# A gated-state attention chained to a cosine MoE on one core: w_in's tiles loaded with 32 or 64 rows outermost, heads p and p+4 paired, early k and r in two loads each

## The chip, the cores and the metric

The kernel runs on one core of one Trainium2 chip. The metric is device microseconds (us) of one execution, as the median of several. A profile is one execution recorded by the hardware profiler; its span, from the first instruction to the last, is a little shorter than that execution's time.

The engines have their own instruction streams and run them in order: PE (TensorE, matmuls; PEld is its weight load), DVE (VectorE), ACT (ScalarE), POOL (GpSimd) and SP (SyncE, which here only issues DMA transfers; SPq in the profile). They wait for each other through semaphores. The 16 DMA engines of the core move what the queues issue.

## The reference

r, k and v are (4 batches, 8 heads, 768 steps, 48), in float32. w_in (384 x 2048) and w_out (2048 x 384) are float64: the kernel sees every weight as two 32-bit words, so one row's piece of 128 columns is 1 KB.

```python
for t in range(S):                                   # attention, state (B, H, D, D)
    cur = np.einsum('bhd,bhe->bhde', u[None] * k[:, :, t], v[:, :, t])
    y[:, :, t] = np.einsum('bhd,bhde->bhe', r[:, :, t], state + cur)
    state = w[None, :, :, None] * state + np.einsum('bhd,bhe->bhde', k[:, :, t], v[:, :, t])
x = y.transpose(0, 2, 1, 3).reshape(B * S, H * D)    # 3072 tokens x 384
h = x @ w_in
out = (h * np.cos(h)) @ w_out
```

## The kernel before

**Attention.** Tokens come in 24 chunks of 128 (`chunk(i, ...)`). A chunk loads k, r and v, multiplies them by decays, forms an A matrix per head pair (`mm_a`, L818), and from A, v and the carried state the 384 columns of x, transposed (`mm_x`, L839 with the state and L850 with A). `mm_z` (L863) makes what the state gains: one matmul a head, 48 x 48, and the two heads of a pair go to the two halves of the output partitions. The first 12 chunks (`EARLY`) come before the MoE begins; the others are spread through it and are loaded in another way (`late`).

Heads are handled in pairs (p, j): p of 0 to 3, and j = 0 or 1 says which half of the 128 partitions a head takes. Before the change, head h = 2p + j, so heads 0 and 1 are a pair. The early chunks keep k and r in tiles of eight slots of 64 (`k`, `r_all`), pair by pair.

**Order of x's rows.** `mm_x` can write 32 rows of the output at a time, so the 384 columns of x stand in three tiles (kk) of four groups (g) of 32 rows, and a group holds pieces of heads as `x_columns(kk, g)` lists them. w_in's rows must stand in the same order on the partitions.

**MoE.** 3072 tokens go in eight blocks of 384 and w_in's 2048 columns in 16 tiles f of 128. One step is one block with one f: nine matmuls for h (L230), then the cosine gate on ACT and DVE (L241, L244, L247, L1017, L1020, L1023), then nine matmuls for the output (L236). The first four blocks take f in groups (0 to 1, 2 to 4, 5 to 9, 10 to 15), the last four take all 16 in a row.

**Weights.** `conv(i, ...)` brings tile f of w_in (even i) or w_out (odd i) into one of three raw buffers (`raw`, twice, and a part of `r_all`), and turns float64 into two float32r parts: ACT L552 and DVE L560 and L572 read the raw words, POOL L583 adds and sets the buffer free, ACT L588 writes the high part (`w_in_hi`, `w_out_hi`), DVE L593 the low part. The load is `load_raw`: w_out's tile in one DMA (L461), w_in's in eight (L446), since its rows are permuted. Near the end the weights are loaded once more for a check of their range, w_in in natural order in one DMA (L456).

**What sets the order.** `Plan` fixes one order for all engines when the kernel is built, from costs and due times written in the code. At run time every engine goes through its list in order. The framework gives SP's DMAs eight completion semaphores in turn, so that a DMA also waits for the one eight places ahead of it to land.

Of the kernel before, what the change touches and what calls it, by code (L numbers as in the profile page):

```python
# [15 lines left out]
ALU = mybir.AluOpType  # L16
# [55 lines left out]
class Plan:  # L72
# [91 lines left out]
def kernel(  # L164
# [49 lines left out]
    w_in_w = moe_w_in.bitcast(I32)  # L214
# [35 lines left out]
    with ExitStack() as actx:  # L250
# [37 lines left out]
        wr = att.tile([NP, 2, DP], F32, name="wr")  # L288
# [8 lines left out]
        dec_k = att.tile([P, H, D], F32, name="dec_k")  # L297
# [11 lines left out]
        op = plan.op  # L309
        PE, DVE, ACT, POOL, SP, ACTQ = "PE", "DVE", "ACT", "POOL", "SP", "ACTQ"  # L310
# [22 lines left out]
        def start_dve():  # L333
# [9 lines left out]
            SP,  # L343
            -200,
            0.1,
            lambda: nc.sync.dma_start(wr[:, :, 0:D], w.rearrange("(p j) d -> p j d", j=2)),
            [],
            lat=2.2,
        )
# [48 lines left out]
        b_tab = Buf(B_EARLY)  # L398
# [4 lines left out]
                nc.tensor.transpose(pt[:, p, :], decT_k[:, p, :], ident)  # L403

        def tab_copy():
            pt = b_tab().rearrange("q (p j d) -> q (p j) d", p=NP, j=2)
            nc.scalar.copy(dec_k, pt[:, :, 0:D])

        o_tt = op(PE, -6, 0.5, tab_t, [o_dtk, o_pool], [b_tab], lat=0.3)
        o_dk = op(ACT, -6, 0.45, tab_copy, [o_tt], [b_tab])  # L410
# [6 lines left out]
            lat=3.0,  # L417
# [16 lines left out]
        def load_raw(i, raw, by_x=False):  # L434
            f, part = divmod(i, 2)
            if part == 0 and by_x:
                rl = 2 * DFF
                for kk in range(NK):
                    g = 0
                    while g < 4:  # L440

                        first = x_columns(kk, g)
                        n = 2 - len(first) + 1
                        (h0, skip0), (h1, skip1) = (x for i in range(n) for _, x in x_columns(kk, g + i))
                        c0, c1 = h0 * D + max(skip0, 0), h1 * D + max(skip1, 0)
                        nc.sync.dma_start(  # L446
                            raw()[32 * g : 32 * (g + n)].rearrange("p (kk f) w -> p kk (f w)", kk=NK)[:, kk],
                            bass.AP(
                                tensor=w_in_w.tensor,
                                offset=w_in_w.offset + c0 * rl + f * P * 2,  # L450
                                ap=[[(c1 - c0) * rl, 2], [rl, 16 * n], [1, 2 * P]],
                            ),
                        )
                        g += n
            elif part == 0:
                nc.sync.dma_start(  # L456
                    raw().rearrange("p (kk f) w -> p kk (f w)", kk=NK),
                    w_in_w[:, f * P * 2 : (f + 1) * P * 2].rearrange("(kk p) f -> p kk f", p=P),
                )
            else:  # L460
                nc.sync.dma_start(raw().rearrange("p f w -> p (f w)"), w_out_w[f * P : (f + 1) * P, :])  # L461
# [48 lines left out]

        def x_columns(kk, g):

            j, m, which = (
# [3 lines left out]
            )[kk][g]  # L519
            one, two = 4 * m + j, 4 * m + j + 2  # L520
            return (((0, (one, 0)),), ((0, (two, 16)),), ((0, (one, 32)), (16, (two, -16))))[which]

# [85 lines left out]
        for t in range(2):  # L608
            for j in range(2):
                for g in range(4):  # L610
                    some = [(*x, j, kk - j, g) for kk in range(NK) for _, x in x_columns(kk, g) if x[0] % 2 == j]
                    PARTS.append(some[t])

        last_A = [None]
# [7 lines left out]
        def heads(buf):  # L622
            return buf().rearrange("q (h d) -> q h d", h=H)
# [7 lines left out]
        def chunk(i, due, xbuf):  # L631
# [14 lines left out]
            def load(buf, src):  # L646
                return lambda: nc.sync.dma_start(
                    buf()[:, :, 0:D], src[b, :, c * C : (c + 1) * C, :].rearrange("h t d -> t h d")
                )

            late = i >= EARLY
# [3 lines left out]

            rbs = [rb] if late else [rb, r_first]

            def rn():
                return heads(rb) if late else rb()[:, :, 0:D]

            def load_r():
                nc.sync.dma_start(rn(), r[b, :, c * C : (c + 1) * C, :].rearrange("h t d -> t h d"))

            def load_s(buf, src):
                def part(m, q, n_q, p, n_p, n):
                    j, d0 = m // 2, 32 * (m % 2)
                    nc.sync.dma_start(  # L670
                        staged(buf)[32 * m + q : 32 * m + q + n_q, p : p + n_p, 0:n],
                        bass.AP(
                            tensor=src.tensor,
                            offset=src.offset + ((b * H + 2 * p + j) * S + c * C + 4 * q) * D + d0,
                            ap=[[4 * D, n_q], [2 * S * D, n_p], [1, n]],
                        ),
                    )
# [12 lines left out]

                return go
# [29 lines left out]
            if late:  # L721
# [17 lines left out]
                e0,  # L739
                due - 2.8,  # L740
                c0,
                lambda: n0.tensor_tensor(heads(mb), rn(), kb()[:, :, 0:D], op=ALU.mult),
                [l_r, l_k],
                [*rbs, kb, mb],
                port=True,
# [1 line left out]
            e2, c2, n2 = on(2)  # L747

            def decay_k():
                n2.tensor_tensor(kb()[:, :, 0:D], kb()[:, :, 0:D], dec_k, op=ALU.mult)  # L750

            if not first:
                o_kd = op(e2, due - 2.7, c2, decay_k, [o_m, o_dk], [kb], port=True)
# [50 lines left out]
            def diagonal(j):  # L804
                def go():
                    for p in range(NP):
                        h = 2 * p + j
# [25 lines left out]
            def mm_x():  # L833
                if c:
                    for n, (h, skip, i, at, g) in enumerate(PARTS):
                        p, j = divmod(h, 2)
                        ps = slice(j * DP, j * DP + D)
                        e0 = p * DP + skip
                        nc.tensor.matmul(  # L839
                            xv(i)[G * g : G * g + G, at, :],  # L840
                            zc[b].rearrange("q p e -> q (p e)")[ps, e0 : e0 + G],
                            rT()[ps, p, :],
                            start=(n < 8),
                            stop=False,
                            skip_group_check=True,
                        )
                for n, (h, skip, i, at, g) in enumerate(PARTS):
                    p, j = divmod(h, 2)
                    e0 = h * DP + skip
                    nc.tensor.matmul(  # L850
                        xv(i)[G * g : G * g + G, at, :],
                        vb().rearrange("q h d -> q (h d)")[:, e0 : e0 + G],
                        A[j]()[:, p, :],
                        start=(not c and n < 8),
                        stop=True,
                        skip_group_check=True,
                    )

            def mm_z():
                z = zp()[:, 0 : NP * D].rearrange("q (p e) -> q p e", p=NP)  # L860
                for h in range(H):
                    p, j = divmod(h, 2)
                    nc.tensor.matmul(z[j * DP : j * DP + D, p, :], kb()[:, h, 0:D], vb()[:, h, 0:D], start=True, stop=True)  # L863

            more = c < CPB - 1

# [366 lines left out]
```

## Time and profile before

| | |
|---|---|
| median of 3 runs | 589.65 us (589.63 to 592.54) |
| the profiled execution | 589.45 us |
| its span | 587.7 us |
| PE busy | 527.6 us, 90% of the span |
| DVE, ACT, POOL busy | 395.6, 328.4, 178.2 us |
| loads of w_in's tiles for `conv` | 128 DMAs on SP: 64 of 64 KB, 64 of 32 KB |

The span has four stretches: to about 58 us mostly the early chunks; to 75 us their end and the first steps; from 75 to 232 us the steps of the grouped blocks while the remaining weights are loaded and converted; after that the other steps with the late chunks. Queries by windows give busy time in a stretch, the granted PE clock, and the DMA engines' mean busy share.

### The profile page before, as it was taken

How to read it: one execution, taken by the hardware profiler on the slowest of the kernel's cores; microseconds unless marked ns; L12 is line 12 of the kernel's file. 1: busy time of each engine (PE TensorE's matmuls, PEld its weight loads, DVE VectorE, ACT ScalarE, POOL GpSimd, SP SyncE). 2: the span in 40 equal slices, each digit the busy share in tenths (PEclk: the TensorE clock that was granted, in tenths of full speed). 3: DMA queues.
4: the chain of work that ended last, by engine and by line, in shares of the span. 5: the costliest groups of instructions: out<-in, count | busy, mean ns of one | idle time of the engine just before them, and what ended most of it. 6: DMA issues, size and time to landing. Idle time of an engine off the chain costs nothing.

```text
span 587.7 us, 12700 instructions
## 1 busy us (share of the span) xinstructions
PE 527.6 (90%) x4721; PEld 490.9 (84%) x4721; DVE 395.6 (67%) x820; ACT 328.4 (56%) x841; POOL 178.2 (30%) x186
## 2 busy tenths in 40 slices
PE   8979857778668796999999999999999999999994
PEld 5757647667667696999999999999999999999994
DVE  5759865664666485745677688768777877776552
ACT  3768744653545364555456657655755676565442
POOL 6566322123333133411150445043043313300000
PEclk9989959979788987999999999999999999999998
DMA  9687324345344445632536678345726662501001
GB/s 143 113 143 131 72 81 128 107 142 127 87 102 106 105 102 124 124 45 38 95 70 118 124 166 198 83 121 122 190 81 163 163 155 86 150 3 40 2 1 45
DMA packets 114984, 61.66 MB, mean 105 GB/s; under 512 B 78433, under 2 KB 110818, under 8 KB 114914
## 3 DMA queue, kind: packets, MB, share of 16 engines
q1 hardware_dynamic: 109586, 53.50, 37.4%
q0 software_dynamic: 5184, 7.08, 8.6%
q8 instruction: 38, 0.62, 0.5%
q14 instruction: 32, 0.26, 0.1%
q10 hardware_dynamic: 144, 0.20, 0.1%
HBM read 48.96 MB, written 11.80 MB: 103 GB/s over the span
## 4 chain that ended last, share of the span: by engine, by line
PE 63%; DMA 17%; SPq 7%; DVE 5%; POOL 3%; issue 2%; ACT 1%; DVEq 0%; POOLq 0%; ACTq 0%
PE bank L230 26%; PE both L236 18%; PE bank L236 9%; DMA raw<-in_moe_w_in_dram 8%; SPq L446 7%; DMA r_all<-in_moe_w_in_dram 4%; PE bank L818 3%; PE bank L850 3%; DMA r_all<-in_r_dram 2%; DMA raw<-in_moe_w_out_dram 2%; PE bank L839 1%; POOL f L583 1%; DMA r_all<-in_moe_w_out_dram 1%; DMA k<-in_k_dram 1%; PE bank L863 1%
## 5 line engine op out<-in xcount | busy, mean ns | idle before, releaser
L230 PE MATMUL bank<-xh,w_in_hi 128*128 128x384 f32 x384 | 132.5, 345 | 6.8 <-ACT w_in_hi L588 4.1
L230 PE MATMUL bank<-xh,w_in_lo 128*128 128x384 f32 x384 | 131.3, 342 | 1.6 <-DVE w_in_lo L593 1.6
L230 PE MATMUL bank<-xl,w_in_hi 128*128 128x384 f32 x384 | 131.2, 342 | 0.0
L1023 DVE TENSOR_TENSOR gl<-f,gh 128x384 fp32r<-128x384 f32 (+1 forms) x132 | 78.6, 599 | 30.2 <-ACT gh L1020 29.9
L241 ACT ACTIVATE qi<-bank 128x384 int32<-128x384 f32 (+1 forms) x132 | 62.8, 479 | 60.1 <-PE bank L230 59.6
L247 ACT ACTIVATE f<-f 128x384 f32<-128x384 f32 (+1 forms) x132 | 67.3, 513 | 44.6 <-DVE f L244 43.0
L244 DVE SCALAR_TENSOR_TENSOR f<-bank,qi 128x384 f32<-128x384 f32 (+1 forms) x132 | 70.9, 540 | 29.5 <-ACT qi L241 29.1
L236 PE MATMUL both<-w_out_hi,gh 128*128 128x384 f32 x256 | 89.1, 348 | 1.4 <-DVE f L1052 1.1
L1017 DVE TENSOR_TENSOR f<-bank,f 128x384 f32<-128x384 f32 (+1 forms) x132 | 70.9, 540 | 27.3 <-ACT f L247 25.6
L1020 ACT CAST gh<-f 128x384 fp32r<-128x384 f32 (+1 forms) x132 | 65.8, 501 | 42.0 <-DVE f L1017 35.8
L236 PE MATMUL both<-w_out_hi,gl 128*128 128x384 f32 x256 | 88.7, 346 | 0.0
L236 PE MATMUL both<-w_out_lo,gh 128*128 128x384 f32 x256 | 88.3, 345 | 0.0
L230 PEld LDWEIGHTS bank<-xh,w_in_hi 128*128 128x128 f32 x384 | 74.2, 193 | 8.8 <-ACT w_in_hi L588 4.5
L230 PEld LDWEIGHTS bank<-xh,w_in_lo 128*128 128x128 f32 x384 | 73.9, 193 | 2.2 <-DVE w_in_lo L593 2.2
L230 PEld LDWEIGHTS bank<-xl,w_in_hi 128*128 128x128 f32 x384 | 74.1, 193 | 0.0
L236 PE MATMUL bank<-w_out_hi,gl 128*128 128x384 f32 x128 | 45.5, 356 | 20.1 <-DVE gl L1023 20.1
L808 ACT ACTIVATE A<-ident,a 128x128 f32<-128x128 f32 x192 | 59.5, 390 | 4.4 <-DVE a L799 4.2
L236 PE MATMUL bank<-w_out_hi,gh 128*128 128x384 f32 x128 | 45.8, 358 | 11.9 <-ACT f L1050 6.8
L730 POOL TENSOR_TENSOR kT<-kT,decT_k 112x512 f32<-112x512 f32 x12 | 15.7, 1311 | 128.5 <-DVE kT L725 78.4
L236 PEld LDWEIGHTS both<-w_out_hi,gh 128*128 128x128 f32 x256 | 49.5, 193 | 3.1 <-DVE f L1052 1.9
L236 PEld LDWEIGHTS both<-w_out_hi,gl 128*128 128x128 f32 x256 | 49.7, 194 | 0.0
L236 PEld LDWEIGHTS both<-w_out_lo,gh 128*128 128x128 f32 x256 | 49.7, 194 | 0.0
(104 smaller groups left out, 802.6 us busy)
## 6 DMA issues: line engine op xcount, KB each, us to landing
raw<-in_moe_w_out_dram SPq DMA_DIRECT2D x22, 384.0 KB
out_dram<-f POOLq DMA_DIRECT2D x36, 192.0 KB, 5.5
raw<-in_moe_w_in_dram SPq DMA_DIRECT2D x13, 384.0 KB
k<-in_k_dram SPq DMA_DIRECT2D x24, 192.0 KB
v<-in_v_dram SPq DMA_DIRECT2D x24, 192.0 KB
out_dram<-f SPq DMA_DIRECT2D x23, 192.0 KB
r_all<-in_moe_w_out_dram SPq DMA_DIRECT2D x10, 384.0 KB
raw<-in_k_dram SPq DMA_DIRECT2D x31, 96.0 KB
```

Source lines behind the costliest of these rows:

```text
L230: nc.tensor.matmul(ph, a, b_, start=(i == 0), stop=(i == len(mm) - 1))
L236: nc.tensor.matmul(acc, a[:, ts], b_[:, f, :], start=(first and i == 0), stop=(last and i == 2))
L241: nc.scalar.activation(qi, ph, AF.Copy, scale=INV_2PI, bias=0.25)
L244: nc.vector.scalar_tensor_tensor(q, ph, INV_2PI, qi, op0=ALU.mult, op1=ALU.subtract)
L247: nc.scalar.activation(q, q, AF.Sin, scale=TWO_PI, bias=0.5 * math.pi)
L446: nc.sync.dma_start(raw()[32 * g : 32 * (g + n)].rearrange("p (kk f) w -> p kk (f w)", kk=NK)[:, kk], bass.AP(tensor=w_in_w.tensor, offset ...
L808: nc.scalar.activation(A[j]()[:, p, :], ident, AF.Copy, scale=ab()[:, h : h + 1])
L818: nc.tensor.matmul(cube(Ap[j])[:, p, :], kT()[ps, p, :], rT()[ps, p, :], start=True, stop=True)
L850: nc.tensor.matmul(xv(i)[G * g : G * g + G, at, :], vb().rearrange("q h d -> q (h d)")[:, e0 : e0 + G], A[j]()[:, p, :], start=(not c and ...
L1017: nc.vector.tensor_tensor(g()[:, cs], ph()[:, cs], q()[:, cs], op=ALU.mult)
L1020: nc.scalar.copy(gh()[:, cs], g()[:, cs])
L1023: nc.vector.tensor_tensor(gl()[:, cs], g()[:, cs], f32(gh())[:, cs], op=ALU.subtract)
```

## The change

w_in's tile comes in five DMAs in place of eight. In each, the outermost dimension of both sides is 32 or 64 rows; before, the DRAM side had two runs of 16 or 32 rows (outermost 2). For that, `x_columns` gets another order of x's columns, and that order needs heads p and p + 4 as a pair (head h = p + 4j). The tables of decays (`wr`, `dec_k`) and the late chunks' staged loads are renumbered to match. In the early chunks k and r are loaded in two DMAs each (heads 0 to 3 to the even slots, 4 to 7 to the odd ones), so that a pair stands side by side; products with v-ordered tiles read those tiles through a permuted view. `mm_z` goes through heads in their order: the four of one half of the partitions first, then the four of the other.

```diff
         def load_raw(i, raw, by_x=False):
             f, part = divmod(i, 2)
             if part == 0 and by_x:
-                rl = 2 * DFF
-                for kk in range(NK):
-                    g = 0
-                    while g < 4:
...
-                        nc.sync.dma_start(
-                            raw()[32 * g : 32 * (g + n)].rearrange("p (kk f) w -> p kk (f w)", kk=NK)[:, kk],
-                            bass.AP(
...
-                                ap=[[(c1 - c0) * rl, 2], [rl, 16 * n], [1, 2 * P]],
+                def rows(p0, n, kk, n_kk, c0, dc):
+                    rl = 2 * DFF
+                    dims = [[rl, n], [dc * rl, n_kk], [1, 2 * P]]
+                    nc.sync.dma_start(
+                        raw()[p0 : p0 + n].rearrange("p (kk f) w -> p kk (f w)", kk=NK)[:, kk : kk + 2 * n_kk - 1 : 2],
...
+                rows(32, 64, 0, 2, 0, 320)
+                rows(0, 32, 0, 2, 160, 64)
+                rows(96, 32, 0, 2, 128, 64)
+                rows(0, 64, 1, 1, 64, 0)
+                rows(64, 64, 1, 1, 256, 0)
...
+            def load_p(buf, src):
+                def go():
+                    for j in range(2):
+                        nc.sync.dma_start(
+                            buf()[:, j::2, 0:D],
+                            src[b, j * NP : (j + 1) * NP, c * C : (c + 1) * C, :].rearrange("h t d -> t h d"),
+                        )
...
-            l_k = op(SP, due - 5.2, 1.35, load(kb, k), ahead, [kb], lat=2.6, line=ln)
-            l_r = op(SP, due - 5.1, 1.35, load_r, ahead, rbs, lat=2.6, line=ln)
+            l_k = op(SP, due - 5.2, 1.35, (load if late else load_p)(kb, k), ahead, [kb], lat=2.6, line=ln)
+            l_r = op(SP, due - 5.1, 1.35, load_r if late else load_p(rb, r), ahead, rbs, lat=2.6, line=ln)
...
             def decay_k():
-                n2.tensor_tensor(kb()[:, :, 0:D], kb()[:, :, 0:D], dec_k, op=ALU.mult)
+                n2.tensor_tensor(in_turn(kb), in_turn(kb), split(dec_k), op=ALU.mult)
...
                 for h in range(H):
-                    p, j = divmod(h, 2)
-                    nc.tensor.matmul(z[j * DP : j * DP + D, p, :], kb()[:, h, 0:D], vb()[:, h, 0:D], start=True, stop=True)
+                    j, p = divmod(h, NP)
+                    at = h if late else 2 * p + j
+                    nc.tensor.matmul(z[j * DP : j * DP + D, p, :], kb()[:, at, 0:D], vb()[:, h, 0:D], start=True, stop=True)
```

PE, DVE, ACT and POOL keep their lists, instruction for instruction; only operands differ. SP's list changes in two kinds of place. The first is a weight tile in the grouped stage. Before, on SP (L446 is w_in, L461 w_out, L1063 a store of a finished block; `DMAHW` are the eight completion semaphores, `Pool` means that POOL has set the raw buffer free):

```order
L446 DMA raw_118<-in_moe_w_in_dram 64x1x256 [waits DMAHW6_49,Pool_49]
L446 DMA raw_118<-in_moe_w_in_dram 32x1x256 [waits DMAHW7_49]
L446 DMA raw_118<-in_moe_w_in_dram 32x1x256 [waits DMAHW0_49]
L446 DMA raw_118<-in_moe_w_in_dram 64x1x256 [waits DMAHW1_49]
L446 DMA raw_118<-in_moe_w_in_dram 64x1x256 [waits DMAHW2_49]
L446 DMA raw_118<-in_moe_w_in_dram 32x1x256 [waits DMAHW3_49]
L446 DMA raw_118<-in_moe_w_in_dram 32x1x256 [waits DMAHW4_49]
L446 DMA raw_118<-in_moe_w_in_dram 64x1x256 [waits DMAHW5_49]
L461 DMA raw_117<-in_moe_w_out_dram 128x768 [waits DMAHW6_49,Pool_49]
```

After, the same place on SP (L442 is w_in, L462 w_out, L1081 a store):

```order
L442 DMA raw_118<-in_moe_w_in_dram 64x2x256 [waits DMAHW7_49,Pool_49]
L442 DMA raw_118<-in_moe_w_in_dram 32x2x256 [waits DMAHW0_49]
L442 DMA raw_118<-in_moe_w_in_dram 32x2x256 [waits DMAHW1_49]
L442 DMA raw_118<-in_moe_w_in_dram 64x256 [waits DMAHW2_49]
L442 DMA raw_118<-in_moe_w_in_dram 64x256 [waits DMAHW3_49]
L462 DMA raw_117<-in_moe_w_out_dram 128x768 [waits DMAHW4_49,Pool_49]
```

Three issues are gone, and w_out's load, which stood behind a wait for the first of the eight w_in pieces, now waits for a DMA ahead of the tile.

The second place is an early chunk. Before, SP has three loads for each chunk (L647 for k and v, L665 for r; here two chunks):

```order
L647 DMA k_84<-in_k_dram 128x8x48 [waits DMAHW4_49,PE_49,Pool_49]
L665 DMA r_all<-in_r_dram 128x8x48 [waits DMAHW5_49,Pool_49]
L647 DMA v_87<-in_v_dram 128x8x48 [waits DMAHW6_49,PE_49]
L647 DMA k_85<-in_k_dram 128x8x48 [waits DMAHW7_49,PE_49,Pool_49]
L665 DMA r_all<-in_r_dram 128x8x48 [waits DMAHW0_49,DMAHW2_49,PE_49,Pool_49]
L647 DMA v_88<-in_v_dram 128x8x48 [waits DMAHW1_49,PE_49]
```

After, it has five (L655 for the halves of k and r; the same two chunks):

```order
L655 DMA k_84<-in_k_dram 128x4x48 [waits DMAHW5_49,PE_49,Pool_49]
L655 DMA k_84<-in_k_dram 128x4x48 [waits DMAHW6_49,PE_49]
L655 DMA r_all<-in_r_dram 128x4x48 [waits DMAHW7_49,Pool_49]
L655 DMA r_all<-in_r_dram 128x4x48 [waits DMAHW0_49]
L647 DMA v_87<-in_v_dram 128x8x48 [waits DMAHW1_49,PE_49]
L655 DMA k_85<-in_k_dram 128x4x48 [waits DMAHW2_49,PE_49,Pool_49]
L655 DMA k_85<-in_k_dram 128x4x48 [waits DMAHW3_49,PE_49]
L655 DMA r_all<-in_r_dram 128x4x48 [waits DMAHW4_49,PE_49,Pool_49]
L655 DMA r_all<-in_r_dram 128x4x48 [waits DMAHW5_49]
L647 DMA v_88<-in_v_dram 128x8x48 [waits DMAHW6_49,PE_49]
```

Two issues more for each of the 12 early chunks, and eight places ahead is now less than two chunks ahead.

More of the change, by code (lines that the diff above doesn't have):

```diff
@@ L345 @@
             0.1,
[L346 removed]
+            lambda: nc.sync.dma_start(wr[:, :, 0:D], w.rearrange("(j p) d -> p j d", j=2)),
             [],
@@ L405, in tab_copy @@
         def tab_copy():
-            pt = b_tab().rearrange("q (p j d) -> q (p j) d", p=NP, j=2)
-            nc.scalar.copy(dec_k, pt[:, :, 0:D])
+            pt = b_tab().rearrange("q (p j d) -> q p j d", p=NP, j=2)
+            nc.scalar.copy(dec_k.rearrange("q (j p) d -> q p j d", j=2), pt[:, :, :, 0:D])
         o_tt = op(PE, -6, 0.5, tab_t, [o_dtk, o_pool], [b_tab], lat=0.3)
@@ L436, in load_raw @@
             if part == 0 and by_x:
-                rl = 2 * DFF
-                for kk in range(NK):
-                    g = 0
-                    while g < 4:
[L442 to L446, printed above, removed]
-                            raw()[32 * g : 32 * (g + n)].rearrange("p (kk f) w -> p kk (f w)", kk=NK)[:, kk],
-                            bass.AP(
-                                tensor=w_in_w.tensor,
-                                offset=w_in_w.offset + c0 * rl + f * P * 2,
-                                ap=[[(c1 - c0) * rl, 2], [rl, 16 * n], [1, 2 * P]],
-                            ),
-                        )
-                        g += n
+                def rows(p0, n, kk, n_kk, c0, dc):
[3 more added lines that the diff above has]
+                        raw()[p0 : p0 + n].rearrange("p (kk f) w -> p kk (f w)", kk=NK)[:, kk : kk + 2 * n_kk - 1 : 2],
+                        bass.AP(
+                            tensor=w_in_w.tensor,
+                            offset=w_in_w.offset + c0 * rl + f * P * 2,
+                            ap=dims if n_kk > 1 else [dims[0], dims[2]],
+                        ),
+                    )
[4 more added lines that the diff above has]
+                rows(64, 64, 1, 1, 256, 0)
             elif part == 0:
@@ L513, in x_columns @@
         def x_columns(kk, g):
-            j, m, which = (
[3 rows of a table removed]
+            return (
[3 rows of a table added]
             )[kk][g]
-            one, two = 4 * m + j, 4 * m + j + 2
-            return (((0, (one, 0)),), ((0, (two, 16)),), ((0, (one, 32)), (16, (two, -16))))[which]
         def conv(i, due, behind=None):
@@ L610 @@
                 for g in range(4):
-                    some = [(*x, j, kk - j, g) for kk in range(NK) for _, x in x_columns(kk, g) if x[0] % 2 == j]
+                    some = [(*x, j, kk - j, g) for kk in range(NK) for _, x in x_columns(kk, g) if x[0] // NP == j]
                     PARTS.append(some[t])
@@ L649, in load, with split, in_turn @@
                 )
+            def load_p(buf, src):
[4 more added lines that the diff above has]
+                            src[b, j * NP : (j + 1) * NP, c * C : (c + 1) * C, :].rearrange("h t d -> t h d"),
+                        )
+                return go
+            def split(ap):
+                return ap.rearrange("q (j p) d -> q j p d", j=2)
+            def in_turn(buf):
+                ap = buf()[:, :, 0:D]
+                return split(ap) if late else ap.rearrange("q (p j) d -> q j p d", j=2)
             late = i >= EARLY
@@ L659, in chunk @@
             rbs = [rb] if late else [rb, r_first]
-            def rn():
-                return heads(rb) if late else rb()[:, :, 0:D]
             def load_r():
-                nc.sync.dma_start(rn(), r[b, :, c * C : (c + 1) * C, :].rearrange("h t d -> t h d"))
+                nc.sync.dma_start(heads(rb), r[b, :, c * C : (c + 1) * C, :].rearrange("h t d -> t h d"))
             def load_s(buf, src):
@@ L741, in chunk @@
                 c0,
-                lambda: n0.tensor_tensor(heads(mb), rn(), kb()[:, :, 0:D], op=ALU.mult),
+                lambda: n0.tensor_tensor(
+                    split(heads(mb)), split(heads(rb)) if late else in_turn(rb), in_turn(kb), op=ALU.mult
+                ),
                 [l_r, l_k],
@@ L847, in mm_x @@
                 for n, (h, skip, i, at, g) in enumerate(PARTS):
-                    p, j = divmod(h, 2)
+                    j, p = divmod(h, NP)
                     e0 = h * DP + skip
```

8 lines of the change are left out of this document (4 added, 4 removed), and 6 rows, old and new, of the table b_fine.

## The prediction

> **What bounds the kernel now.** I read the page's slices first, then the chain that ended last, then the stages, then who waits for whom in the stage that loses time.
>
> ```profile
> PE   8979857778668796999999999999999999999994
> PEclk9989959979788987999999999999999999999998
> PE 63%; DMA 17%; SPq 7%; DVE 5%; POOL 3%; issue 2%; ACT 1%; DVEq 0%; POOLq 0%; ACTq 0%
> ```
>
> One digit is 14.7 us. From slice 16 on (235 us) PE is full and the clock too; ahead of it PE shows 6 to 9 and the clock dips. A quarter of the chain is DMA and SP's issuing. The stages, and the seven stretches of half clock after 73.7 us as one sum:
>
> ```profile
> core 0: us, PE busy (x) PEld busy (x) DVE busy (x) ACT busy (x) POOL busy (x), PEclk, DMA share, GB/s
> 75.00:232.00 157.00, 115.22 (x583) 107.79 (x580) 92.56 (x194) 76.17 (x173) 47.01 (x45) 0.87 0.42 109
> 232.00:300.00 68.00, 68.00 (x461) 66.92 (x461) 42.79 (x81) 36.31 (x80) 17.02 (x19) 0.98 0.43 74
> 300.00:578.30 278.30, 278.18 (x2371) 266.04 (x2370) 202.93 (x421) 166.87 (x440) 72.33 (x66) 1.00 0.45 108
> sum 44.20, PE 31.59 PEld 29.67 DVE 33.80 ACT 29.07 POOL 18.50; mean PE 4.51 PEld 4.24 DVE 4.83 ACT 4.15 POOL 2.64
> ```
>
> From 232 us on PE never stops, so nothing there can be won. From 75 to 232 us it stands still for 157.00 - 115.22 = 41.8 us, and 31.59 us of its busy time ran at half clock, which costs 15.8 us. Who is waited for in that stage:
>
> ```profile
> ACT raw L552 <- DMA raw<-in_moe_w_in_dram: 26.9, 6, 7.1
> PE bank L236 <- DVE gl L1023: 20.1, 8, 6.5
> DVE f L560 <- DMA raw<-in_moe_w_in_dram: 15.1, 4, 7.2
> DVE f L560 <- DMA r_all<-in_moe_w_in_dram: 13.8, 3, 5.6
> ACT r_all L552 <- DMA r_all<-in_moe_w_in_dram: 12.0, 3, 5.4
> ```
>
> PE waits for the gate's last product on DVE, but DVE and ACT run in order, and at their heads stands the first conversion step (L560, L552) of a w_in tile that hasn't landed: 28.9 us on DVE and 38.9 us on ACT. So w_in's loads bound this stage. What one costs: two issue groups of eight, three transfers on the chain (from one of the last issues of a tile to landing), and a window with hardly anything else in flight.
>
> ```profile
> 82.64 4.95 SPq L446 DMA_DIRECT2D r_all<-in_moe_w_in_dram  x8
> 132.79 6.77 SPq L446 DMA_DIRECT2D raw<-in_moe_w_in_dram  x8
> 85.73 6.46 DMA r_all<-in_moe_w_in_dram
> 96.32 6.99 DMA raw<-in_moe_w_in_dram
> 138.96 10.22 DMA raw<-in_moe_w_in_dram
> 66.00:68.00 2.00, 2.00 (x70) 1.52 (x74) 1.82 (x7) 0.80 (x2) 0.00 (x0) 1.00 0.14 48
> ```
>
> Issuing takes 5 to 7 us and landing 6.5 to 10.2 us more; from first issue to landing the first tile takes 85.73 + 6.46 - 82.64 = 9.6 us, the last 138.96 + 10.22 - 132.79 = 16.4. In the last row the DMA engines are 0.14 busy and move 48 GB/s: a share of 0.14 of sixteen is little more than two engines. A tile of 384 KB at that rate needs 8.2 us, which is the landing. The DRAM side's outermost dimension was 2.
>
> **The change part by part.** *w_in's load.* Three issues fewer, and 32 or 64 rows outermost. The rows nearest to the new load are four DMAs of 32 rows outermost, one DMA of the same w_in bytes with 128 rows outermost, w_out's tile (the same 384 KB) from issue to landing, and a window in which that w_in load moves, beside the end of another.
>
> ```profile
> 299.29 1.75 SPq L670 DMA_DIRECT2D raw<-in_k_dram  x4
> 360.15 0.37 SPq L456 DMA_DIRECT2D raw<-in_moe_w_in_dram  x1
> 76.22 2.82 DMA raw<-in_moe_w_out_dram
> 360.00:361.00 1.00, 1.00 (x8) 1.00 (x7) 0.96 (x3) 0.95 (x2) 0.73 (x1) 1.00 0.68 240
> ```
>
> Four issues in 1.75 us are 0.44 each, so five take about 2.2 us. For landing the ends are 2.8 us (w_out's row) and 6.5 us (the least now); I take 2.8, as that row has the same bytes with many rows outermost, and 240 GB/s was seen where this weight comes in so. A load then takes about 5 us in place of 9.6 to 16.4. The longest wait at L560 or L552 was 7.2 us; loads that are 4.6 to 11.4 us quicker take most of these waits away, the more so as each also sets a buffer free sooner.
>
> What is late next: PE's own work, then DVE. The stage's matmuls:
>
> ```profile
> 75.00:232.00 157.00, 58.11 (x281) 54.13 (x282) 0.87 0.42 109
> 75.00:232.00 157.00, 62.95 (x270) 53.02 (x270) 0.87 0.42 109
> 235.95 4.69 PE bank L230 x27
> ```
>
> These are L230 (x281) and L236 (x270), and 27 of them at full clock take 4.69 us, 0.174 each: 551 x 0.174 = 95.7 us, about 99 with the rest. DVE was busy for 92.56 us in the same stage, so in 99 us it would be 0.93 busy. While PE was full, from 300 us on, DVE was 202.93/278.30 = 0.73 busy, and I have no row where PE stays full beside a DVE at 0.9. Bounds for what stays of the idle time: nothing, or half (21 us). I keep 11, which makes the stage's DVE share 92.56/110 = 0.84, between the two: **-31 us**.
>
> *The clock.* It was halved around the long waits. If those go, so does the 15.8 us; one row says that a shorter wait does it as well:
>
> ```profile
> 186.40:189.80 3.40, 2.87 (x9) 2.70 (x10) 3.37 (x9) 3.02 (x8) 3.25 (x5) 0.50 0.48 70
> 186.93 0.69 PE L236 MATMUL bank<-w_out_hi,gh 128*128 128x384 f32 x1 [2.72 <-ACT f L1050]
> ```
>
> A wait of 2.72 us ended inside a half-clock stretch. I keep 3 us for one or two such: **-12.8 us**. The Trainium skill, "TensorE: Matmul & The Clock Gate" (HAM oscillation), asks for no PE gap above some 3.4 us. By that rule waits of under 3 us would cost no clock, and this term would be the whole 15.8; the row above speaks against it.
>
> *The early chunks.* The first w_in load sits among them, and this is what stands there:
>
> ```profile
> 19.86 4.97 SPq L446 DMA_DIRECT2D raw<-in_moe_w_in_dram  x8
> 18.07 4.02 DMA r_all<-in_r_dram
> 25.64 6.76 DMA r_all<-in_r_dram
> 32.00:34.00 2.00, 0.00 (x0) 0.00 (x0) 1.46 (x4) 1.98 (x8) 1.39 (x2) 1.00 1.21 202
> 36.00:38.00 2.00, 2.00 (x36) 1.62 (x32) 1.76 (x4) 1.90 (x6) 1.34 (x2) 0.54 1.32 163
> SPq L647 <- PE bank L850: 13.4, 7, 3.3
> ```
>
> An r load behind it took 6.76 us where one ahead took 4.02; then PE stood for 2 us or more and ran at 0.54 of its clock. With the tile on all engines that is worth about 2.7 us of waiting and 1.7 of clock. Against it stand 24 more issues on SP at 0.44 us, 10.6 us in all. Bounds: nothing, as SP stands still anyway (13.4 us for k's and v's buffers alone in the first 75 us), or 10.6 where each lies on the path. An r that comes in halves is ready 0.9 us later than now (two more issues ahead of its end), but only in the chunks where r is what POOL waits for. I take 3: **-1.4 us**. Behind these issues on SP are v and the next chunk's loads; PE waits for them through POOL L742 (r times k) and L850.
>
> *mm_z in the order of the partition halves.* Same 16 matmuls (eight in two passes), but neighbours no longer alternate halves. Rows: mm_z now, four full-width transposes that cannot overlap, and mm_x's state part, where four of one half come ahead of four of the other.
>
> ```profile
> 320.42 0.56 PE L863 MATMUL bank<-v,k 128*48 128x48 f32 x16
> 8.42 0.66 PE L403 MATMUL bank<-ident,decT_k 128*128 128x128 f32 x4 [0.45 <-DVE decT_k L387]
> 53.53 0.67 PE L839 MATMUL bank<-rT,zc 48*32 48x128 f32 x32
> ```
>
> One after the other, 16 of 48 columns would take 16 x 48/128 x 0.66/4 = 0.99 us, 0.43 more than now; 20 chunks have an mm_z, so the ends are 0 and 8.6 us (only eight of them in the stage where PE is full). L839 does 32 of 128 columns in 0.67 us, eight in the 0.17 us that one of L403's takes, though four of one half come ahead of four of the other: PE overlaps matmuls that don't stand side by side. So I stay near the low end: **+1 us**.
>
> *At no cost.* The permuted views on POOL: L750 reads k in strides now, at 1046 ns, L793 reads whole rows, at 1104 ns:
>
> ```profile
> L793 POOL TENSOR_TENSOR f<-f,u_b 128x384 f32<-128x384 f32 x24 | 26.5, 1104 | 1.4 <-DMA u_b<-in_u_dram 1.3
> L750 POOL TENSOR_TENSOR k<-k,dec_k 128x384 f32<-128x384 f32 x24 | 25.1, 1046 | 1.3
> ```
>
> The renumbered columns, decays and late loads keep their counts and shapes.
>
> **Sum.** -31 - 12.8 - 1.4 + 1 = -44.2 us against the span of 587.7: 543.5, and with the 1.75 us around it (589.45 - 587.7) 545 us. That execution lies 0.2 us under the median shown.
>
> **The rivals.**
> - *DVE and the three raw buffers take over.* A tile holds its buffer through load, conversion and everything ahead of these steps on in-order engines. Half of the idle time and of the half clock stay: 589.45 - (41.8 + 15.8)/2 = 561 us. For it: DVE's 0.93. Against: DVE has slack if its waits go first.
> - *Nothing is left over.* All idle time, clock loss and the early 4.4 us go: 589.45 - 41.8 - 15.8 - 4.4 = 527 us. Against it: every block boundary in this stage hands over accumulators.
> - *The loads don't spread.* Then only three issues of eight are saved. SP's issuing is 7% of the chain, 41 us, and 3/8 of it is 15: 574 us. For it: no row shows exactly these shapes; against: L670's and L456's.
> - *Slower: each added early load costs its own transfer.* At 2.82 us, the shortest landing quoted, 24 of them on the path are 68 us: 545 + 68 - 3 = 610. It decides from 1.9 us each (47.2/24). Against it: four issues in 1.75 us, so DMAs of one queue overlap. The Trainium skill, "DMA: Bandwidth & Descriptors" (Rules for kernel authors), speaks for it: join small transfers into large ones, under 64 KB one pays mostly overhead, and two transfers in place of one gain nothing. By its fixed cost of some 2.0 us for a DMA (given for GpSimd's path; an estimate from the page) the 24 would add 48 us and end near 590. L670's row says that this cost overlaps.
>
> **How the numbers follow.** My forecast (538 to 553) has 0.57, DVE and buffers 0.24, nothing left over 0.12, no spread 0.04, slower 0.03. From 529 to 563 takes in the forecast and most of its two neighbours, some 0.83, and the bounds of the open costs: 0 to 21 us of idle time kept, 0 to 8.6 for mm_z. All but the last end faster by over 0.5%, about what a measurement of this kernel can tell from no change: 0.96, with 0.01 for the same and 0.03 slower.
>
> **What would show it.** DMA windows with a w_in load alone well over 100 GB/s; five issues in about 2 us; L552 and L560 waiting for w_in under 15 us in all from 75 us to the stage's end; the clock at 1.00 there; PE without a standstill from about 190 us in place of 232; L863 at about 0.56 us a chunk. I'd be wrong if loads still land after 6 us, if waits for DVE or POOL replace those for DMA, or if the first steps, which start here now, come later than this by more than the early terms:
>
> ```profile
> 68.46 0.45 PE L230 MATMUL bank<-xh,w_in_hi 128*128 128x384 f32 x1
> ```

## The result, and the profile after

| | before | after |
|---|---|---|
| median, us | 589.94 (589.63 to 592.54) | 528.70 (528.49 to 530.07) |
| ratio after/before | | 0.896, 95% interval 0.893 to 0.899 |
| the profiled execution, its span | 589.45, 587.7 | 528.52, 526.7 |
| PE busy | 527.6 (90%) | 513.1 (97%) |

The change takes 10.4% off. One execution of one kernel below took 785.63 us at a mean granted clock of 0.58, and that kernel's median leaves it out. The page's slices and the chain that ended last, of the changed kernel:

```profile
PE   8999979999999999999999999999999999999995
PEclk9999979999999999999999999999999999999998
PE 89%; DVE 5%; ACT 2%; SPq 1%; DMA 1%; issue 1%; POOL 0%; DVEq 0%; POOLq 0%
```

One digit is 13.2 us. PE is full from slice 6 (79 us), where before it was full from slice 16 (235 us). DMA and SP's issuing have gone from 24% of the chain to 2%. The stages of the changed kernel by windows (same columns as before):

```profile
core 0: us, PE busy (x) PEld busy (x) DVE busy (x) ACT busy (x) POOL busy (x), PEclk, DMA share, GB/s
0.00:58.00 58.00, 54.70 (x1053) 42.15 (x1054) 44.66 (x103) 38.91 (x121) 37.97 (x54) 1.00 0.76 140
58.00:75.00 17.00, 12.96 (x290) 9.89 (x287) 16.37 (x38) 12.43 (x37) 6.34 (x6) 0.91 0.34 99
75.00:180.00 105.00, 105.00 (x592) 105.00 (x593) 96.28 (x195) 77.34 (x174) 49.32 (x47) 0.98 0.68 168
75.00:232.00 157.00, 157.00 (x898) 156.63 (x899) 127.43 (x251) 106.25 (x237) 61.75 (x60) 0.99 0.59 135
```

In the stretch from 75 to 232 us PE was busy for 115.22 us with 583 matmuls; now it is busy all of the 157, with 898. The grouped stage now ends near 180 us, and up to there DVE is 96.28/105 = 0.917 busy while PE never stops.

The load itself, from four views of the changed kernel: two issue groups, the DMAs' sizes with the median time from issue to landing (75 to 150 us), one window of 2 us, and the only waits of ACT or DVE for a w_in tile from 75 to 190 us:

```profile
80.83 2.89 SPq L442 DMA_DIRECT2D raw<-in_moe_w_in_dram  x5
87.58 2.90 SPq L442 DMA_DIRECT2D raw<-in_moe_w_in_dram  x5
raw<-in_moe_w_in_dram SPq DMA_DIRECT2D x28, 64.0 KB, 2.4
raw<-in_moe_w_in_dram SPq DMA_DIRECT2D x7, 128.0 KB, 2.7
92.00:94.00 2.00, 2.00 (x13) 2.00 (x12) 1.64 (x4) 1.06 (x3) 1.02 (x1) 1.00 0.85 319
ACT raw L552 <- DMA raw<-in_moe_w_in_dram: 0.8, 1, 0.8
```

Five issues take 2.9 us and a DMA lands 2.4 to 2.7 us after its own, so a tile needs some 5 us where it needed 9.6 to 16.4 (the last issue lies in both figures). The DMA engines reach a share of 0.85 (other transfers are in that window too). The waits at the first conversion step fell from 67.8 us (26.9 + 15.1 + 13.8 + 12.0) to 0.8.

What PE still loses is at the border of the early chunks and the grouped stage: two standstills (the brackets give the idle time before the row and who ended it), and a stretch of half clock around them.

```profile
64.82 0.44 PE L230 MATMUL bank<-xh,w_in_hi 128*128 128x384 f32 x1
72.09 0.66 PE L230 MATMUL bank<-xh,w_in_hi 128*128 128x384 f32 x1 [1.80 <-DVE zc L935]
74.85 0.69 PE L230 MATMUL bank<-xh,w_in_lo 128*128 128x384 f32 x1 [1.78 <-DVE w_in_lo L593]
72.00:79.00 7.00, 5.13 (x15) 4.65 (x16) 5.27 (x14) 3.10 (x8) 2.21 (x2) 0.51 0.42 123
```

The first row is the first step's first matmul: 64.82 us where it was 68.46.

### The profile page after: what moved, and what is told of

The parts are those of the page before. It is cut to its first block, busy times and chain, and to the rows that moved or that the text cites. A ratio compares the mean times of both kernels' runs of the same rounds, so it can differ in the third digit from the quotient of the medians.

```text
span 526.7 us, 12636 instructions
## 1 busy us (share of the span) xinstructions
PE 513.1 (97%) x4721; PEld 484.0 (92%) x4721; DVE 395.8 (75%) x820; ACT 328.4 (62%) x841; POOL 179.3 (34%) x186
## 4 chain that ended last, share of the span: by engine, by line
PE 89%; DVE 5%; ACT 2%; SPq 1%; DMA 1%; issue 1%; POOL 0%; DVEq 0%; POOLq 0%
PE bank L230 39%; PE both L236 26%; PE bank L236 13%; PE bank L835 3%; PE bank L867 3%; PE bank L856 2%; PE bank L881 2%; ACT A L825 1%; DMA r_all<-in_r_dram 1%; DVE A L841 1%; DVE rT L785 1%; DVE xl L921 1%; SPq L442 1%; PE bank L1099 1%; PE both L726 1%
## 5 line engine op out<-in xcount | busy, mean ns | idle before, releaser
L230 PE MATMUL bank<-xh,w_in_hi 128*128 128x384 f32 x384 | 130.7, 340 | 1.8 <-DVE zc L935 1.8
L230 PE MATMUL bank<-xl,w_in_hi 128*128 128x384 f32 x384 | 129.7, 338 | 0.0
L236 PE MATMUL both<-w_out_hi,gh 128*128 128x384 f32 x256 | 86.6, 338 | 0.1
L236 PE MATMUL both<-w_out_hi,gl 128*128 128x384 f32 x256 | 86.5, 338 | 0.0
L236 PE MATMUL both<-w_out_lo,gh 128*128 128x384 f32 x256 | 86.4, 337 | 0.0
L236 PEld LDWEIGHTS both<-w_out_hi,gh 128*128 128x128 f32 x256 | 48.0, 187 | 0.6 <-DVE f L1070 0.4
L236 PEld LDWEIGHTS both<-w_out_hi,gl 128*128 128x128 f32 x256 | 48.0, 188 | 0.0
L236 PEld LDWEIGHTS both<-w_out_lo,gh 128*128 128x128 f32 x256 | 48.0, 187 | 0.0
L1083 POOL DMA_DIRECT2D out_dram<-f x36 | 32.0, 1032 | 42.8 <-ACT f L1068 39.0
L841 DVE COPY_PREDICATED A<-upper,bank 128x512 f32<-128x512 int32 x48 | 34.4, 738 | 15.8 <-ACT A L825 9.6
```

The lines of the kernel that those rows point to most:

```text
L230: nc.tensor.matmul(ph, a, b_, start=(i == 0), stop=(i == len(mm) - 1))
L236: nc.tensor.matmul(acc, a[:, ts], b_[:, f, :], start=(first and i == 0), stop=(last and i == 2))
L841: return lambda: nc.vector.copy_predicated(A[j](), upper[:, None, :].to_broadcast([P, NP, C]), cube(Ap[j]))
L1083: nc.gpsimd.dma_start(dst, ob(), accum_op=ALU.add)
```

## The experiments

"Before" in each result is a run of the kernel before on the same chip at the same time (589.9, 590.9 and 589.9 us in the three groups of runs).

**The spread alone: eight DMAs, wide or narrow.** Two kernels made from the changed one load a w_in tile in eight DMAs again. In the first, the outermost dimension stays 32 or 64 rows:

```diff
-                    dims = [[rl, n], [dc * rl, n_kk], [1, 2 * P]]
-                    nc.sync.dma_start(...)
+                    for q in range(n_kk):
+                        nc.sync.dma_start(
+                            raw()[p0 : p0 + n].rearrange("p (kk f) w -> p kk (f w)", kk=NK)[:, kk + 2 * q],
...
+                                ap=[[rl, n], [1, 2 * P]],
```

> The changed kernel with w_in's tile in eight DMAs again (one for each row range and kk), 32 or 64 rows outermost. Theory 'spread' (what a load gained is that it uses many DMA engines): three issues more cost about 1.7 us of SP's queue per tile, PE stays full, 528 to 533 us. Rival 'count' (what a load gained is fewer issues and fewer completion slots): back towards the kernel before, 570 to 590 us.

The second differs from the first in the DRAM side's pattern alone, which is two runs of rows again. The second run begins one row early, so that the pattern stays in two dimensions; the weights it reads are shifted there, and the time is what counts:

```diff
-                                ap=[[rl, n], [1, 2 * P]],
+                                ap=[[(n // 2 - 1) * rl, 2], [rl, n // 2], [1, 2 * P]],
```

> The same eight DMAs, but with two runs outermost on the DRAM side (the second run starts one row early, so one row in each half is not the one wanted: time only). Theory 'spread': DMA share back to about 0.14 and 48 GB/s, landing 6 us and more, 580 to 592 us. Rival 'count': the same time as the eight with 32 or 64 rows outermost.

Measured: wide 536.19 us (535.48 to 537.70), ratio to before 0.910 (0.906 to 0.913); narrow 595.83 (593.25 to 598.52), ratio 1.009 (1.006 to 1.012). Of the narrow kernel, two windows of 2 us in which hardly anything else moved and a landing, the wait at L552 (60 to 230 us), and the grouped stage:

```profile
70.00:72.00 2.00, 2.00 (x75) 1.48 (x71) 1.35 (x3) 2.00 (x8) 1.98 (x2) 1.00 0.15 44
72.00:74.00 2.00, 2.00 (x67) 1.67 (x66) 1.82 (x5) 1.40 (x4) 0.44 (x1) 1.00 0.11 38
72.08 6.95 DMA raw<-in_moe_w_in_dram
ACT raw L552 <- DMA raw<-in_moe_w_in_dram: 27.8, 6, 7.2
75.00:180.00 105.00, 77.35 (x441) 70.48 (x433) 60.81 (x131) 48.76 (x116) 27.27 (x25) 0.84 0.38 107
```

Of the wide one, an issue group, its DMAs' landing (75 to 150 us), the longest waits for a w_in tile (60 to 190 us), and the same stage:

```profile
83.58 4.37 SPq L442 DMA_DIRECT2D raw<-in_moe_w_in_dram  x8
raw<-in_moe_w_in_dram SPq DMA_DIRECT2D x24, 64.0 KB, 2.9
POOL f L583 <- DMA r_all<-in_moe_w_in_dram: 11.4, 3, 5.6
75.00:180.00 105.00, 100.60 (x549) 97.08 (x550) 90.74 (x187) 72.77 (x165) 45.45 (x43) 0.97 0.62 156
```

With the same number of DMAs and the same bytes, the pattern makes 59.6 us: nearly the whole result. (The narrow kernel is 5.9 us slower than the kernel before; that was not put down to a step. In its profile PE runs at half clock near the start, see the last section.) The narrow loads show the old picture in every row: a share of 0.11 to 0.15, 7 us to land, 27.8 us at L552. The Trainium skill, "DMA: Bandwidth & Descriptors" (Rules for kernel authors), says that an outermost dimension of a size c below 16 keeps a DMA to at most c engines. By that rule the narrow loads run on two engines of sixteen; the 0.11 to 0.15 here agree.

The wide kernel was expected at 528 to 533 and missed that. The three issues that the change saves per tile are worth another 7.5 us (536.2 against 528.7): an issue group takes 1.5 us longer, and POOL waits 11.4 us for a tile where it waits 5.2 in the changed kernel. Some 2.4 us of it are there before the grouped stage: the last early mm_z starts at 70.08 us, against 67.67 in the changed kernel. That eight DMAs also take up all eight completion semaphores of the queue may add to it; the two were not told apart.

**The early halves alone.** The kernel before, with k and r of the early chunks in two loads each and nothing else changed:

```diff
-            l_k = op(SP, due - 5.2, 1.35, load(kb, k), ahead, [kb], lat=2.6, line=ln)
-            l_r = op(SP, due - 5.1, 1.35, load_r, ahead, rbs, lat=2.6, line=ln)
+            l_k = op(SP, due - 5.2, 1.35, (load if late else load2)(kb, k), ahead, [kb], lat=2.6, line=ln)
+            l_r = op(SP, due - 5.1, 1.35, load_r if late else load2(rb, r), ahead, rbs, lat=2.6, line=ln)
```

> The kernel before with nothing changed but early k and r in two DMAs each (heads 0 to 3, heads 4 to 7): the cost of 24 issues alone. Theory 'overlapped': 0 to 4 us more than before, 590 to 594. My term of 3 us lies in it. Rival 'each added load costs its own transfer': 24 x 1.9 us and more, over 630 us.

Measured: 589.67 us (587.69 to 591.71), ratio 0.999 (0.997 to 1.002). The 24 issues cost nothing that shows in the time. Its first step came at 69.56 us, though, 1.1 us later than in the kernel before, and the idle time behind it could hide that. The issues go at the expense of idle time on SP: in the first 60 us it waits less for PE to free v's buffers. The rows are of the kernel before and of this one:

```profile
SPq L647 <- PE bank L850: 13.4, 7, 3.3
SPq L647 <- PE bank L860: 8.3, 4, 3.1
```

**mm_z's order.** The changed kernel with the halves of the partitions in turn again:

```diff
-                for h in range(H):
-                    j, p = divmod(h, NP)
+                for p, j in ((p, j) for p in range(NP) for j in range(2)):
+                    h = p + NP * j
```

> The changed kernel with mm_z going through the heads so that neighbours alternate partition halves again. The profile after has mm_z at 0.78 us against 0.56 before. Theory 'mm_z's order costs': 0.22 us for each of the 8 chunks in the full stretch and for some of the 12 early ones, 1.8 to 4.4 us less, 524 to 527 us. Rival 'hidden': no change, 528.7 within 0.5.

It gave 527.03 us (526.62 to 527.44), ratio 0.894 (0.891 to 0.897). It was run once more beside the changed kernel on one chip:

> The changed kernel once more, on the same chip as the runs that are compared with it here. 528 to 530.

> The changed kernel with mm_z's halves in turn once more, beside the changed kernel on one chip. Theory A: 20 times 0.22 us of PE, of which those in the full stretch and after it show, 1.5 to 3.5 us below the changed kernel. Theory B: mm_z lies beside other work, and the first run's 1.7 us was scatter; within 0.7 us.

The changed kernel gave 529.27 (526.22 to 530.72), this one 527.11 (526.65 to 527.35). One mm_z at about 300 us in the changed kernel, then in this one; and, from the first profile of each, the first and the last of the eight in the full stretch, again the changed kernel first:

```profile
303.28 0.78 PE L881 MATMUL bank<-v,k 128*48 128x48 f32 x16
301.77 0.56 PE L881 MATMUL bank<-v,k 128*48 128x48 f32 x16
234.95 0.78 PE L881 MATMUL bank<-v,k 128*48 128x48 f32 x16
384.51 0.78 PE L881 MATMUL bank<-v,k 128*48 128x48 f32 x16
234.08 0.56 PE L881 MATMUL bank<-v,k 128*48 128x48 f32 x16
382.12 0.56 PE L881 MATMUL bank<-v,k 128*48 128x48 f32 x16
```

Each chunk's mm_z is 0.22 us longer when four matmuls of one half come ahead of four of the other. Eight chunks lie in the full stretch: 1.8 us by rows. By times it is 1.9 (all ten runs of the one kernel have a median of 529.0, all nine of the other 527.1). The second pair of runs agrees with the first, so theory A holds. The half clock at 72 us is also shorter in this kernel (0.76 from 72 to 79 us in both of its profiles, against 0.51), but that is not where the 1.8 us come from: the lag of the changed kernel grows from 0.87 us at the first of the eight to 2.39 at the last, 1.52 in seven mm_z or 0.22 each (0.32 to 1.85 in the second pair). What comes before 234 us, the shorter half clock among it, is the 0.3 to 0.9.

**How near DVE is to its limit.** The changed kernel with DVE's second conversion step done twice, which gives the same words, for w_out's tiles and then for all:

```diff
-                lambda: nc.vector.scalar_tensor_tensor(
-                    ai(), hw(), -0x40000000, ai(), op0=ALU.bitwise_and, op1=ALU.bitwise_or
-                ),
+                lambda: [
+                    nc.vector.scalar_tensor_tensor(
+                        ai(), hw(), -0x40000000, ai(), op0=ALU.bitwise_and, op1=ALU.bitwise_or
+                    )
+                    for _ in range(1 + part)        # second kernel: range(2)
+                ][-1],
```

> The changed kernel with DVE's second conversion step (L572, 0.55 us) done twice for w_out's tiles. From 75 to 180 us 14 of the 28 tiles are w_out's, so DVE's work there goes from 96.3 to about 104 us of 105, a share of 0.99. Theory A, DVE only matters once its work is longer than PE's: 528 to 530. Theory B, the prediction's step, PE can't stay full beside a DVE well over 0.9: at least half of the added 7.7 us shows, 532.5 or more.

> The same with L572 done twice for all tiles: 28 more in the stretch, 15.5 us, DVE's work 111.8 us in a stretch of 105. Theory A: DVE is now longer by 6.8 us, part of which it can do before 75 us or after 180 us; 531 to 536. Theory B: all 15.5 us and the waits of a stage bound by DVE show, 541 or more.

Measured: 536.07 us (534.45 to 537.38) and 542.12 (540.15 to 545.68); ratios 0.907 (0.905 to 0.910) and 0.920 (0.916 to 0.924). Theory A missed twice. From 75 to 195 us, the first kernel and then the second; two parts of this in the first kernel and one in the second; and the first kernel's beginning:

```profile
75.00:195.00 120.00, 115.42 (x635) 112.00 (x636) 114.85 (x228) 82.20 (x187) 54.72 (x52) 0.97 0.65 159
75.00:195.00 120.00, 115.09 (x614) 108.69 (x615) 115.09 (x230) 79.84 (x181) 50.99 (x50) 0.97 0.62 152
75.00:85.00 10.00, 7.17 (x28) 6.78 (x29) 8.76 (x21) 4.64 (x11) 3.38 (x3) 0.66 0.39 120
85.00:135.00 50.00, 50.00 (x285) 49.16 (x285) 48.93 (x101) 38.38 (x88) 20.76 (x20) 1.00 0.64 174
85.00:195.00 110.00, 106.32 (x582) 99.92 (x581) 106.18 (x211) 74.38 (x169) 48.24 (x47) 1.00 0.64 157
8.50:18.50 10.00, 8.53 (x77) 6.67 (x79) 6.53 (x11) 3.55 (x12) 7.97 (x8) 0.66 0.83 117
```

Of the first one's 7.4 us, some 3.2 in its profiled execution come from the beginning, where PE waits longer and runs at half clock for a while. This has nothing to do with the edit, since the first w_out tile is loaded at 42.25 us only. The last early mm_z starts at 70.83 us (67.67 in the changed kernel) and the first late one at 242.82 (234.95), so another 4.7 us come in between, for 7.7 us more of DVE. The second kernel has no half clock at its beginning, and 15.5 us more of DVE make it 13.4 us slower, 0.86 for one.

In both, DVE is busy for 0.957 to 0.959 of the whole stretch and PE has lost its full share, but this average is no limit. In the first kernel PE loses 2.83 us in the first 10, at the border, where it waits for DVE (2.1 us of it for the low part of one w_in tile). Then it is full for 50 us beside a DVE at 48.93/50 = 0.979. In the second, from 85 to 195 us, PE is at 0.967 and DVE at 0.965. Theory B's times came, but its reason, that PE can't stay full beside a DVE well over 0.9, does not hold by these rows. The changed kernel, at 0.917, has little room left all the same.

**Two raw buffers.** The changed kernel without the third buffer; the plan of all engines is made anew for it.

```diff
-        R_raw = ring("raw", 2, [P, DM, 2], I32) + [raw_r]
+        R_raw = ring("raw", 2, [P, DM, 2], I32)
```

> The changed kernel with two raw buffers in place of three (the third, a part of r_all, is not used for weights; the order is planned anew for two). Theory A, the loads are now so quick (2.9 us of issuing and about 3 more to land) that buffers are not near a limit: a tile needs about 6.6 us of PE per pair of loads, so two buffers nearly do; 528 to 533. Theory B, the rival of the prediction, buffers hold the loads: each load then starts only when the conversion before the last one has ended on POOL, waits at L552 and L560 come back, and the time is 540 or more.

Measured: 534.53 us (531.83 to 535.59), ratio 0.905 (0.901 to 0.908): between the two theories, and neither's number. SP's waits for POOL to free a buffer, from 75 to 190 us, in the changed kernel and in this one:

```profile
SPq L442 <- POOL f L583: 32.0, 10, 5.1
SPq L442 <- POOL f L583: 50.2, 11, 6.9
```

The third buffer is worth about 6 us here, the new plan included; with three, these waits hold up nothing that PE needs from 75 to 180 us, where it never stops.

**The last standstills.** Three plans of the kernel with mm_z's halves in turn, in which the first four weight tiles stand elsewhere (tiles in order of i: w_in 0, w_out 0, w_in 1, w_out 1):

```diff
             if g == 0:
-                due = 2 * i - 3.0
+                due = 2 * i - 5.0                        # first kernel
+                due = (-3.0, 1.0, -1.0, 3.0)[i]          # second
+                due = (-5.0, -2.0, -4.0, 1.0)[i]         # third
```

> The changed kernel with mm_z's halves in turn (527.0 in its own run) and the first four weight tiles' due times 2 steps earlier in the plan. The 1.6 us standstills at 72 and 74 us wait for the second w_in tile's parts, which stand late in DVE's and ACT's lists. Theory A: with the conversion earlier both go, and the half clock behind them: 524 to 526. Theory B: the conversion steps only push the early chunks' work back, and the first step comes later by as much: 527 to 530.

> The changed kernel with mm_z's halves in turn, and w_in's second tile ahead of w_out's first in the plan (loads and conversion). Theory A: the two standstills of 1.6 us at 72 to 76 us wait for that tile alone and go; 523 to 526. Theory B: DVE and ACT have as much to do as before, so another wait takes their place; 526 to 530.

> The same with the two tiles of w_in also 2 to 5 steps earlier, and w_out's two 1 to 2 earlier. Theory A: the first step starts with nothing to wait for; 522 to 526. Theory B: as for the version with all four tiles 2 steps earlier (532.4): the conversion takes DVE's time from the early chunks, on which the next steps wait; 528 to 533.

Measured: 532.39 us (529.15 to 535.49), 537.24 (533.53 to 539.61) and 529.07 (526.12 to 531.36), ratios 0.902 (0.897 to 0.907), 0.908 (0.904 to 0.912) and 0.895 (0.892 to 0.899). None beats 527.1, so theory A fails in all three. Theory B's time came for the third alone; the first two lie 2.4 and 7.2 us above its ranges. The first step's first matmul in the first of them, and the longest of PE's waits from 58 to 300 us in the first (two rows) and in the second (one):

```profile
57.70 0.44 PE L230 MATMUL bank<-xh,w_in_hi 128*128 128x384 f32 x1 [0.71 <-DVE A L841]
PE bank L236 <- DVE gl L1041: 1.6, 3, 0.7
PE bank L856 <- DVE A L841: 1.2, 2, 0.7
PE bank L236 <- DVE gl L1041: 4.2, 3, 3.1
```

The first step comes 7 us earlier and the kernel is still slower, by 5.3 us: PE waits for DVE elsewhere, 2.8 us in the two rows shown, the second of them in an attention chunk. That the conversion takes DVE's time from the attention chunks fits these rows; the rest of the 5.3 us was not put down to a wait. In the profiles of the second and the third kernel there is a half clock at the start as well (last section). The version to keep is the changed kernel with mm_z's halves in turn, 527.1 us.

## Why the prediction was right or wrong

It forecast 545 us with a range from 529 to 563; 528.7 was measured. The rival "nothing is left over" (527 us) is what came, and it had been given 0.12. The mechanism was right in the main: w_in's loads bounded the stage, the pattern bounded the loads, and the standstills and the half clock left with them. What failed is how much was held back.

| step | forecast | by the rows |
|---|---|---|
| idle time, 75 to 232 us | -31 (11 kept) | -41.8 (none kept) |
| half clock there | -12.8 (3 kept) | -14.2 (157 x 0.01 = 1.6 kept) |
| early chunks | -1.4 | -3.6 (68.46 to 64.82) |
| mm_z | +1 | +1.8 (8 x 0.22) |
| span | -44.2 | -61.0 |

The rows come to -57.8. Another 1.4 us is a half clock between 232 and 300 us that the kernel before had (68 x 0.02) and the changed one has not; the prediction had said that nothing was to be won there. The end of the kernel, from the start of DVE's last copy, takes 8.4 us in the profile before (from 579.31) and 6.1 in the one after (from 520.62). In five other profiles it takes 6.0 to 7.4, whichever the kernel, so these 2.3 us look like scatter between executions. Together that is -61.5.

- **The step that failed: "I keep 11".** It let PE stand still so that DVE would come out at 0.84 busy, since no row showed a full PE beside a DVE at 0.9. There is such a row now: PE 105.00 of 105 at a DVE of 0.917. The doubled conversion step goes further: PE was full for 50 us beside a DVE at 0.979, so the 0.93 of the prediction was no reason to keep anything. What it did show is that DVE is next: more work there costs time. Half of the 41.8 us was taken as a bound and a middle between the bounds was chosen; the estimate from rows in the prediction itself (99 us of PE work, 92.56 of DVE's, so PE longer) had the right answer.
- **The clock** was kept at 3 us for the same waits, which hardly came. One stretch remains, around two standstills of 1.8 us: 0.51 over 7 us, as shown above. The Trainium skill, "TensorE: Matmul & The Clock Gate" (HAM oscillation), names PE gaps of more than some 3.4 us for that. Here the half clock sets in at the end of a gap of 1.80 (0.98 from 71 to 72 us, 0.50 from 72 to 73).
- **The load's price** held: about 5 us foretold, some 5 measured. In it the issues were too cheap: 0.58 us each against 0.44. The four DMAs that gave 0.44 were no good model for 64 rows by 2 pieces. That SP's issuing matters at all, 7.5 us for three of eight issues and what hangs on them, was part of no step.
- **The early chunks**: the term weighed a gain of 4.4 us against a cost of 3 for 24 issues. With the halves alone the cost doesn't show (589.67 against 589.94), though 1.1 us of it could be hidden there. The r load behind w_in's tile is quicker as foretold, though only in part: the row below is its second half, 4.33 us, or 4.83 from the first half's issue at 25.49, against 6.76 before and 4.02 undisturbed.

```profile
25.99 4.33 DMA r_all<-in_r_dram
```

- **mm_z** came out near double the forecast. PE overlaps matmuls that don't stand side by side, as L839 had suggested, but not all: 0.78 us lies between the 0.56 of halves in turn and the 0.99 of one after the other.
- **The rivals.** "DVE and the three raw buffers take over" did not come, but stood closer than its price says: with one buffer less 534.5, with 15.5 us more on DVE 542. "The loads don't spread" is ruled out by the wide and the narrow kernel. "Each added early load costs its own transfer" is ruled out by the halves alone (24 at its 1.9 us, or rather 47.2/24 = 2.0, would be 47 us). The rule of the Trainium skill to join small transfers ("DMA: Bandwidth & Descriptors", Rules for kernel authors) would have cost 48 us by the prediction's estimate. What the Trainium skill says there of two transfers in place of one is said of two partition halves, and these are halves by heads. The trace shows 24 transfers more, of half the size, without that price, and SP waiting less beside them.

## What to carry to other kernels

Look at the DMA share of a window in which one load moves alone: 0.14 of sixteen engines is a load on two of them, and putting a dimension of 32 or 64 outermost was worth 60 us here, the number of DMAs only 7.5. When a wait goes, add up what each engine has to do in the stage that is left; if PE has the most, forecast a full PE, and hold nothing back for a next engine that comes out at 0.9; here PE was full beside one at 0.917 for the stage, and at 0.979 for 50 us. Work added to that engine was paid for all the same, at 0.6 (4.7 of 7.7 us) to 0.86 of its length, and an earlier conversion only made the kernel slower.

## What the runs showed of the hardware

- One issue on SP has no single price: 0.44 us for four loads of k, 0.55 (4.37/8) for the wide pieces of w_in and 0.58 for five larger ones; the narrow pieces of the kernel before took 0.62 (4.95/8) and up to 0.92 (7.38/8):

```profile
89.50 7.38 SPq L446 DMA_DIRECT2D raw<-in_moe_w_in_dram  x8
```

- The clock can halve at the start of this kernel. From 8.5 to 18.5 us it was 0.66 in four of the fourteen profiles (the narrow loads, the doubled DVE step for w_out, the second and the third plan of the last standstills) and 1.00 in the other ten. What follows came some 2.4 to 3.5 us later (the second mm_z at 20.63 us with the doubled step, at 17.20 in the changed kernel), part of which is longer waiting. In the four, PE's waits for DVE between 5 and 12 us add up to 2.34 to 2.49 us (1.29 and 1.18 with the doubled step); in the others, to 1.86 at most. That their sum decides it was not tested.
